# The last row block of an output projection, loaded in groups of 25 rows on a decode kernel

## The chip, the cores and the metric

The kernel runs on one core of a Trainium2 chip. The metric is device time in microseconds for one execution, the median of the runs. Five engines work side by side, each with its own instruction queue: TensorE (PE; its weight loads are shown as PEld), VectorE (DVE), ScalarE (ACT), GpSimd (POOL) and SyncE (SP). Sixteen DMA engines move data between HBM and SBUF; here SP issues the large loads and ACT a few tiny ones and the store. An instruction waits on semaphores, and a load raises its own semaphore as it lands, a step for each DMA engine that carried a share of it.

## The reference

One decode step for one token with D = 576: a layer norm, then two branches on the same normalised row, summed with the residual.

```python
xn = _layernorm(x)
# A: 32 query heads on 16 key/value heads, the last W = 4096 positions of the cache
q = xn @ wq                                  # 576 x 4096
p = softmax(q k^T * 128**-0.5)               # per head, 4096 keys
a = (p v) reshaped to 4096 @ wo              # 4096 x 576
# B: a gated MLP with one token
z = gelu(xn @ w_in)                          # 576 x 4608, halves z1, z2
b = (z1 * (w_sp * layernorm(z2) + b_sp)) @ w_out   # 2304 x 576
return x + a + b
```

All tensors are bfloat16. About 51 MB are read in one execution: the two caches' windows (16.8 MB each), wq, w_in, w_out and wo.

## The kernel before

The order of the work is written out by hand: every engine runs its instructions in the order in which the program names them. SP's queue is a list of loads. `rows` (L74 to L83) loads n row blocks of a weight matrix, `load_kv` (L85 to L89) four heads of a cache. A weight matrix with R rows lies in SBUF with R/128 consecutive rows to each of the 128 partitions, so that "row block" s is the 128 rows `p * (R/128) + s`, one to a partition. Four large buffers a, b, c, d (32 KB in each partition) are reused, and a load into one waits for the last reader of what was there.

SP's order is: wq in two loads, K0, K1, w_in in two, K2, V0, K3, V1, V2, V3, w_out, and then wo (32 row blocks, wo's row `32 p + s`) in five loads of 14, 9, 6, 2 and 1 blocks (L108), so that the last blocks can be used soon after they land. A row block of wo is 1152 bytes in a partition. Eight semaphores serve all the loads and the store in turn, so the ninth load waits for the first to have landed, and so on.

The stages: x is normalised (POOL computes the power -0.5, L203) and put into a stationary form `XT`; wq gives q, and a set of copies with masks spreads it as `Qb`. For each of four groups of four heads: `keys` transposes K on DVE (L264), `scores` multiplies on TensorE (L271), `sm_a` and `sm_b` do the softmax (exp on ACT, transposes on DVE, copies on ACT), `pv` multiplies with V, and `tail` normalises (`norm`), brings the result into columns with `y_mms` and copies it to `Y` (L363). `Y` has, for each of 32 row blocks of wo, a column of 128 values with a column of zeros on either side; a pair of columns is the stationary operand, so the output row falls into one of the two rows of an accumulator.

At the end, `out_mms` (L468 to L472) multiplies one row block with its column of `hv` (branch B) or `Y` (branch A): four matmuls of 144 columns, for the four quarters of the 576 outputs, into two accumulators `acc` of 2 x 144 that lie in different column groups of TensorE. Order on TensorE after the last `pv`: 12 blocks of w_out (`out_hv(0)`, `out_hv(1)`), the transposition of the last group's result, six more blocks of w_out, then the 32 blocks of wo in the order of their loads. DVE and ACT copy one accumulator each (L486, L487), and ACT issues the store (L488).

POOL clears tiles at the start (`pz` in L166 is the longest) and does the two powers.

Of the kernel before, what the change touches and what calls it, by code (L numbers as in the profile page):

```python
# [8 lines left out]
FP32 = mybir.dt.float32  # L9
BF16 = mybir.dt.bfloat16  # L10
# [4 lines left out]
D = 576  # L15
HQ = 32
HKV = 16
DH = 128
# [6 lines left out]
TP = W // 32  # L25
TC = TP // 2
NR = 98
NF = FH // 128
QW = D // 4
XP = D // 3  # L30
EPS = 1e-5
SCALE = DH ** -0.5
# [5 lines left out]
def kernel(  # L38
# [14 lines left out]
    nc = tc.nc  # L53
    P = nc.NUM_PARTITIONS
# [3 lines left out]
    big = ctx.enter_context(tc.tile_pool(name="big", bufs=1))  # L58
    const = ctx.enter_context(tc.tile_pool(name="const", bufs=1))
# [5 lines left out]
    ps_m = ctx.enter_context(tc.tile_pool(name="ps_m", bufs=1, space=bass.MemoryType.PSUM))  # L65
# [8 lines left out]
    def rows(slot, src, name, lo, n, at=None):  # L74

        w = src.shape[1]
        if at is None:
            t = big.tile([P, n * w], BF16, name=f"{name}{lo}", tag=slot)[:]
        else:
            t = slot[:, at:at + n * w]  # L80
        v = t.rearrange("p (s c) -> p s c", c=w)
        nc.sync.dma_start(v, src.rearrange("(p s) c -> p s c", p=P)[:, lo:lo + n, :])  # L82
        return [(lo + s, v[:, s, :]) for s in range(n)]  # L83

    def load_kv(slot, src, g, name):  # L85

        t = big.tile([P, TP * DH], BF16, name=f"{name}{g}", tag=slot)
        nc.sync.dma_start(t[:], src[0, GK * g:GK * g + GK, SK - W:SK, :].rearrange("h (r t) d -> r h (t d)", t=TP))
        return t[:].rearrange("p (t d) -> p t d", d=DH)  # L89

    wq_h = A_wq.rearrange("r (e c) -> (r e) c", e=2)
    win_h = B_w_in.rearrange("r (e c) -> (r e) c", e=2)
    K, V = {}, {}
    rest = big.tile([P, TP * DH], BF16, name="rest", tag="d")
    wq_sb = rows(rest, wq_h, "wq", 0, 2, 0) + rows("a", wq_h, "wq", 2, 7)
    K[0] = load_kv("b", A_k_cache, 0, "k")
    K[1] = load_kv("c", A_k_cache, 1, "k")
    win_sb = rows("a", win_h, "win", 0, 7) + rows(rest, win_h, "win", 7, 2, 4096)
    K[2] = load_kv("b", A_k_cache, 2, "k")
    V[0] = load_kv("c", A_v_cache, 0, "v")  # L100
    K[3] = load_kv("d", A_k_cache, 3, "k")
    V[1] = load_kv("a", A_v_cache, 1, "v")
    V[2] = load_kv("b", A_v_cache, 2, "v")
    V[3] = load_kv("c", A_v_cache, 3, "v")
    ends = [big.tile([P, TP * DH], BF16, name=f"end{n}", tag="ad"[n]) for n in range(2)]
    wout_sb = rows(ends[0], B_w_out, "wout", 0, NF, 0)
    wo_sb = []
    for n, t, at in ((14, 1, 0), (9, 1, 14), (6, 0, NF), (2, 0, NF + 6), (1, 0, NF + 8)):  # L108
        wo_sb += rows(ends[t], A_wo, "wo", len(wo_sb), n, at * D)


    xrow = const.tile([1, D], BF16, name="xrow")
    for n in range(3):
        nc.scalar.dma_start(xrow[:, XP * n:XP * (n + 1)], x_flat[:, XP * n:XP * (n + 1)])
    spb = const.tile([1, 2], BF16, name="spb")
# [4 lines left out]
    ident = const.tile([P, P], BF16, name="ident")  # L120
# [47 lines left out]
    for n in range(2):  # L168
        t = ps_s.tile([P, 2, 512], FP32, name=f"S{n}")
# [9 lines left out]
    nc.gpsimd.memset(mb[:], 0.0)  # L179

    xtw = const.tile([1, NS, D // NS, 2], BF16, name="xtw")
    nc.vector.tensor_copy(xtw[:], xrow[:].rearrange("p (m j) -> p j m", j=NS).unsqueeze(3).to_broadcast([1, NS, D // NS, 2]))  # L184
    for j in range(NS):
        nc.tensor.matmul(ps_x[:, j:j + 1], lhsT=xtw[:, j].rearrange("p m h -> p (m h)"), rhs=ones_b[:, 0:1],  # L186
                         start=True, stop=True)
# [30 lines left out]
    for s, wv in wq_sb:  # L218
        for g in range(4):
            nc.tensor.matmul(  # L220
                qps[32 * g:32 * g + 2, :], lhsT=XT[:, s, :], rhs=wv[:, 512 * g:512 * (g + 1)],
                start=(s == 0), stop=(s == NS - 1), tile_position=(0, 32 * g),
# [12 lines left out]
    for k in range(4):  # L235
        for be in range(4):
            nc.tensor.matmul(
                qps2[:, k, be, :].rearrange("p (r g) -> p r g", r=2),
                lhsT=q_rep[0:NR, 2 * k + be // 2, be % 2].rearrange("p a d -> p (a d)"),
                rhs=idq, start=True, stop=True)  # L240
# [10 lines left out]
    Y = const.tile([P, 32, 3], BF16, name="Y")  # L251
    nc.gpsimd.memset(Y[:], 0.0)
    hv = const.tile([P, NF, 3], BF16, name="hv")
    nc.gpsimd.memset(hv[:], 0.0)
    KT = {}
    st = {}

    def keys(g, c):
# [4 lines left out]
        for n in range(4):  # L263
            nc.vector.transpose(dst[:, 1024 * n:1024 * (n + 1)], src[:, 1024 * n:1024 * (n + 1)])  # L264
        KT[g, c] = kT

    def scores(g, c):
        kv = KT.pop((g, c))[:].rearrange("p (t s) b r x e -> p b e x t r s", s=2)
        for be in range(4):
            for x in range(GK):  # L270
                nc.tensor.matmul(  # L271
                    S[g % 2][32 * x:32 * x + 8, c, :],
                    lhsT=Qb[:, GK * g + x, be].rearrange("p a h -> p (a h)"),
                    rhs=kv[:, be // 2, be % 2, x],
                    start=(be == 0), stop=(be == 3), tile_position=(0, 32 * x),
                )
# [141 lines left out]
    def tail(g):  # L418
        recip(g)
        norm(g)  # L420
        y_mms(g)
        y_copy(g)
# [16 lines left out]
    acc = []  # L439
    for n, pool in enumerate((ps_a, ps_b)):  # L440
        t = pool.tile([P, 512], FP32, name=f"acc{n}", tag="ab"[n])
        acc.append(t[32 * n:32 * n + 2, 0:QW])
        for r in range(2):
            nc.tensor.matmul(acc[n], lhsT=one3[:, 1 - r:3 - r], rhs=xrow[:, QW * (2 * r + n):QW * (2 * r + n + 1)],
                             start=(r == 0), stop=False, tile_position=(0, 32 * n))
# [19 lines left out]
    sums(3)  # L465
    pv(3)

    def out_mms(lhs, col, wv, last):  # L468
        for r in range(2):
            for n in range(2):  # L470
                nc.tensor.matmul(acc[n], lhsT=lhs[:, col, 1 - r:3 - r], rhs=wv[:, QW * (2 * r + n):QW * (2 * r + n + 1)],  # L471
                                 start=False, stop=(last and r == 1), tile_position=(0, 32 * n))  # L472

    def out_hv(c):
        for t, wv in wout_sb[6 * c:6 * c + 6]:
            out_mms(hv, t, wv, False)

    out_hv(0)
    out_hv(1)
    tail(3)  # L480
    out_hv(2)
    for t, wv in wo_sb:
        out_mms(Y, t, wv, t == 31)

    res = const.tile([2, 2 * QW], BF16, name="res")
    nc.vector.tensor_copy(res[:, 0:QW], acc[0])  # L486
    nc.scalar.copy(res[:, QW:2 * QW], acc[1])  # L487
    nc.scalar.dma_start(out.rearrange("a b (r c) -> (a b r) c", r=2), res[:])  # L488
# [30 lines left out]
```

## Time and profile before

| | |
|---|---|
| median of 3 runs | 127.01 us (126.64 to 127.16) |
| the profiled execution | 126.97 us, span of its instructions 125.1 us |
| bytes read | 50.96 MB, 407 GB/s over the span |
| busy: PE, DVE, ACT, POOL | 70.2, 78.6, 43.2, 7.2 us |
| DMA packets | 2613, of those 2592 on SP's queue |
| mean granted TensorE clock | 0.754; 1.00 after 116 us |
| wo's one-block load, issue to landing | 31.2 us |

How to read it: times in the profile are microseconds from the first instruction. The page gives busy time by engine and in 40 equal slices, the DMA queues, the chain of work that ended last, and groups of instructions by source line. Further views list the instructions in order of time, who waited for whom, and busy time in chosen stretches: for each engine the busy time and the number of instructions, then the granted clock, the mean busy share of the 16 DMA engines, and GB/s. In a line such as `117.31 3.06 PE L471 ...` the first number is the start and the second the length; the brackets hold the idle time before it and what ended that. Beside these views the trace keeps a record of every DMA packet (queue, start, length, bytes) and of every step of a load's semaphore.

### The profile page before, as it was taken

Reading aid. Unit: us, or ns where it says so; the run is one execution under the profiler, and the core shown is the slowest. Engines: PE = TensorE matmul, PEld = TensorE weight load, DVE = VectorE, ACT = ScalarE, POOL = GpSimd, SP = SyncE. Lnnn points to the kernel's source line nnn. Section 1 sums busy time; section 2 is a strip of 40 time slices with the busy share of each in tenths; the row PEclk is TensorE's granted clock in tenths of the full one; section 3 lists DMA queues with packets and bytes.
Section 4 is the critical chain, followed back from the end, with each engine's and each line's share of the span. In section 5 each row is a group of like instructions: output and inputs, shape, how many; then the busy total and the mean of one; then the engine's idle time right before and its main releaser. Section 6 shows DMA issues by size and latency. Waiting matters only on the chain.

```text
span 125.1 us, 1826 instructions
## 1 busy us (share of the span) xinstructions
PE 70.2 (56%) x728; PEld 30.4 (24%) x728; DVE 78.6 (63%) x152; ACT 43.2 (34%) x101; POOL 7.2 (6%) x21
## 2 busy tenths in 40 slices
PE   0012841009886659999580991059892931059972
PEld 0011201001101002999100031002212311026961
DVE  6845135899699976509999367999938359003200
ACT  2100011000000974998079009608701941940000
POOL 2972000000000000000000000000000100000000
PEclk9999997555599958655568599558997555555999
DMA  4999899998999999898999989899998989999960
GB/s 113 507 422 440 363 503 409 430 482 356 498 389 433 385 482 471 377 492 341 492 430 419 471 367 487 359 482 440 409 482 356 492 374 453 414 434 409 413 248 0
DMA packets 2613, 51.06 MB, mean 408 GB/s; under 512 B 300, under 2 KB 430, under 8 KB 686
## 3 DMA queue, kind: packets, MB, share of 16 engines
q1 hardware_dynamic: 2592, 50.96, 95.3%
q8 instruction: 5, 0.08, 0.2%
q14 instruction: 2, 0.02, 0.0%
q10 hardware_dynamic: 14, 0.00, 0.0%
HBM read 50.96 MB, written 0.00 MB: 407 GB/s over the span
## 4 chain that ended last, share of the span: by engine, by line
DMA 62%; DVE 30%; PE 4%; SPq 1%; issue 1%; ACT 0%; DVEq 0%
DMA k<-in_A_k_cache_dram 36%; DMA end<-in_A_wo_dram 25%; DVE kT L264 22%; DVE pt L309 4%; PE S L271 3%; SPq L82 1%; DVE mx L292 1%; DVE on L349 1%; DVE om L345 1%; PE acc L471 0%; PE yps L356 0%; DVE rs L326 0%; ACT res L487 0%; DVE mt L281 0%; DVE mb L287 0%
## 5 line engine op out<-in xcount | busy, mean ns | idle before, releaser
L271 PE MATMUL S<-kT,Qb 128*8 128x512 bf16 x128 | 32.4, 1145 | 23.2 <-DVE kT L264 22.7
L264 DVE STREAM_TRANSPOSE kT<-k 128x1024 f32<-128x1024 f32 x32 | 36.8, 1207 | 6.2 <-DMA k<-in_A_k_cache_dram 6.2
L298 ACT ACTIVATE pz<-S,nm 32x1024 bf16<-32x1024 f32 x16 | 19.2, 1198 | 34.0 <-DVE nm L295 21.1
L312 ACT COPY PT<-pt 32x128 f32<-32x128 f32 x64 | 19.9, 311 | 16.5 <-DVE pt L309 15.8
L335 PE MATMUL ops<-v,PT 128*32 128x512 bf16 x128 | 11.0, 506 | 6.8 <-ACT PT L312 6.8
L271 PEld LDWEIGHTS <-Qb 128*8 128x8 bf16 x128 | 3.6, 96 | 44.9 <-issue 35.4
L309 DVE STREAM_TRANSPOSE pt<-pz 128x1024 f32<-128x1024 f32 x8 | 9.4, 1210 | 0.8 <-ACT pz L298 0.8
L345 DVE SCALAR_TENSOR_TENSOR om<-ops,rs,dmask 128x512 f32<-128x512 f32 x4 | 3.0, 751 | 10.5 <-PE ops L335 10.3
L371 PEld LDWEIGHTS <-win 128*128 128x128 bf16 x126 | 7.9, 166 | 2.0 <-issue 2.0
L371 PE MATMUL zps<-XT,win 128*128 128x2 bf16 x126 | 8.0, 202 | 0.0
L292 DVE TENSOR_REDUCE mx<-S 128x1 f32<-128x1024 f32 x4 | 4.9, 1216 | 4.0 <-PE S L271 3.9
L335 PEld LDWEIGHTS <-PT 128*32 128x32 bf16 x128 | 3.8, 118 | 11.4 <-ACT PT L312 6.9
L229 ACT CAST q_rep<-qps 128x512 bf16<-128x512 f32 x2 | 1.2, 585 | 14.9 <-DVE q_rep L231 14.9
L410 POOL TENSOR_TENSOR mz<-mz,mhalf 128x1 f32<-128x1 f32 x1 | 0.6, 553 | 84.9 <-DVE mz L409 84.9
L186 PE MATMUL ps_x<-ones_b,xtw 1*128 1x1 bf16 x9 | 0.4, 162 | 8.9 <-DVE xtw L184 8.9
L471 PE MATMUL acc<-end,Y 128*2 128x144 bf16 x128 | 4.5, 226 | 0.9 <-DMA end<-in_A_wo_dram 0.8
L231 DVE CAST q_rep<-qps 128x512 bf16<-128x512 f32 x2 | 1.4, 692 | 4.9 <-PE qps L220 4.2
L487 ACT CAST res<-acc 2x144 bf16<-2x144 f32 x1 | 0.3, 270 | 12.0 <-PE acc L471 12.0
L471 PEld LDWEIGHTS <-Y 128*2 128x2 bf16 x128 | 4.1, 84 | 1.2 <-issue 1.2
L356 PE MATMUL yps<-on,sel 128*32 128x32 f32 x32 | 2.0, 210 | 4.1 <-DVE on L349 4.1
L349 DVE TENSOR_REDUCE on<-om 128x128 f32<-128x512 f32 x4 | 4.2, 1043 | 0.1
L486 DVE CAST res<-acc 2x144 bf16<-2x144 f32 x1 | 0.3, 295 | 5.7 <-PE acc L471 5.7
(96 smaller groups left out, 57.6 us busy)
## 6 DMA issues: line engine op xcount, KB each, us to landing
k<-in_A_k_cache_dram SPq DMA_DIRECT2D x4, 4096.0 KB
v<-in_A_v_cache_dram SPq DMA_DIRECT2D x4, 4096.0 KB, 25.4
win<-in_B_w_in_dram SPq DMA_DIRECT2D x1, 4032.0 KB, 26.9
wq<-in_A_wq_dram SPq DMA_DIRECT2D x1, 3584.0 KB, 12.8
end<-in_B_w_out_dram SPq DMA_DIRECT2D x1, 2592.0 KB, 22.3
end<-in_A_wo_dram SPq DMA_DIRECT2D x1, 2016.0 KB
end<-in_A_wo_dram SPq DMA_DIRECT2D x1, 1296.0 KB
rest<-in_B_w_in_dram SPq DMA_DIRECT2D x1, 1152.0 KB
```

Of the source, the lines that this page charges most:

```text
L264: nc.vector.transpose(dst[:, 1024 * n:1024 * (n + 1)], src[:, 1024 * n:1024 * (n + 1)])
L271: nc.tensor.matmul(S[g % 2][32 * x:32 * x + 8, c, :], lhsT=Qb[:, GK * g + x, be].rearrange("p a h -> p (a h)"), rhs=kv[:, be // 2, be % 2, x],
L292: nc.vector.tensor_reduce(out=mx[:, 0:1], in_=s[:], op=ALU.max, axis=mybir.AxisListType.XY)
L298: nc.scalar.activation(pz[lo:hi, :, :, x, :], s[lo:hi].rearrange("p a (t r e) -> p (a t) r e", r=8, e=2), ACT.Exp, bias=nm[lo:hi, 0:1], sc ...
L309: nc.vector.transpose(dst[:, 1024 * n:1024 * (n + 1)], src[:, 1024 * n:1024 * (n + 1)])
L312: nc.scalar.copy(PT4[32 * a:32 * a + 32, :, x, :], pt[32 * x:32 * x + 32, :, 2 * a:2 * a + 2])
L335: nc.tensor.matmul(ops[32 * q:32 * q + 32, :], lhsT=d["PT"][:, t0 // 2:t0 // 2 + 2].rearrange("p t x h e -> p (t x h e)"), rhs=V[g][:, t0: ...
L345: nc.vector.scalar_tensor_tensor(out=om[:].rearrange("p c d -> p (c d)"), in0=ops[:], scalar=d["rs"][:, 0:1], in1=dmask[:].rearrange("p c ...
L349: nc.vector.reduce_sum(on[:], om[:].rearrange("p c d -> p d c"), axis=AXX)
L356: nc.tensor.matmul(yps[32 * g:32 * g + 32, :], lhsT=sel[:, dq, :], rhs=d["on"][:, 32 * dq:32 * dq + 32], start=(dq == 0), stop=(dq == 3), ...
L371: nc.tensor.matmul(zps[:, :, t], lhsT=wt[:, t, :], rhs=XT[:, s, :], start=(s == 0 and t == 0), stop=(s == NS - 1 and t == NF - 1), skip_gr ...
L471: nc.tensor.matmul(acc[n], lhsT=lhs[:, col, 1 - r:3 - r], rhs=wv[:, QW * (2 * r + n):QW * (2 * r + n + 1)], start=False, stop=(last and r ...
```

## The change

The last row block of wo (block 31) is no longer one load of 128 rows. Its first quarter of columns (144 of 576) comes with block 30, which lies just before it in memory: a load of 128 rows of 720 columns, 1440 bytes. Block 29 gets its own load, and is now the last block that TensorE multiplies. The other three quarters of block 31 (432 columns, 864 bytes a row) go to a tile `ext` of its own, with three slots of 432 columns: 125 of the 128 rows in five loads of 25 rows, to partitions 0 to 24 and 80 to 104 of the slots in turn, issued last of all on SP; the remaining three rows in loads of one row each, to partitions 80 to 82 of the third slot, issued early, between K1 and w_in. `ext` is cleared by POOL before that.

As row `i` of the block now lies in another partition, Y's column 31 has to follow. `move` holds three 128 x 128 matrices with a one for each row that moved and zeros elsewhere (POOL copies them out of the identity); three matmuls bring the column into three columns `yx`, DVE copies them to `Yx`, which has zeros on either side like `Y`. Each slot of `ext` is then multiplied with its column of `Yx`, three quarters each: nine matmuls. The partitions without a row have zeros on both sides.

`out_mms` is split so that one quarter can be issued alone (`out_mm`). The loads from w_in on stand further down in the source, behind the definition of `ext`; apart from the three small loads their order on SP is the same.

```diff
+XR = 25
+XB = 80
+XN = 3
...
-    for n, t, at in ((14, 1, 0), (9, 1, 14), (6, 0, NF), (2, 0, NF + 6), (1, 0, NF + 8)):
-        wo_sb += rows(ends[t], A_wo, "wo", len(wo_sb), n, at * D)
...
+    ext = const.tile([P, XN, D - QW], BF16, name="ext")
+    nc.gpsimd.memset(ext[:], 0.0)
+    last = A_wo.rearrange("(p s) c -> p s c", p=P)[:, 31, QW:D]
+    for i in range(P - 5 * XR):
+        nc.sync.dma_start(ext[XB + i:XB + i + 1, 2, :], last[5 * XR + i:5 * XR + i + 1])
+    win_sb = rows("a", win_h, "win", 0, 7) + rows(rest, win_h, "win", 7, 2, 4096)
...
+    for n, t, at in ((14, 1, 0), (9, 1, 14), (6, 0, NF)):
+        wo_sb += rows(ends[t], A_wo, "wo", len(wo_sb), n, at * D)
+    wo_p = A_wo.rearrange("(p s) c -> p (s c)", p=P)
+    at, w30 = (NF + 6) * D, D + QW
+    nc.sync.dma_start(ends[0][:, at:at + w30], wo_p[:, 30 * D:30 * D + w30])
+    row30 = ends[0][:, at:at + w30]
+    row29 = ends[0][:, at + w30:at + w30 + D]
+    nc.sync.dma_start(row29, wo_p[:, 29 * D:30 * D])
+    for j in range(5):
+        lo = XB * (j % 2)
+        nc.sync.dma_start(ext[lo:lo + XR, j // 2, :], last[XR * j:XR * j + XR])
...
+    Yx = const.tile([P, XN, 3], BF16, name="Yx")
+    nc.gpsimd.memset(Yx[:], 0.0)
+    move = const.tile([P, XN, P], BF16, name="move")
+    nc.gpsimd.memset(move[:], 0.0)
+    for j in range(6):
+        lo, n = XB * (j % 2), min(XR, P - XR * j)
+        nc.gpsimd.tensor_copy(move[:, j // 2, lo:lo + n], ident[:, XR * j:XR * j + n])
...
+    def out_mm(lhs, col, q, wv, last=False):
+        n, r = q % 2, q // 2
+        nc.tensor.matmul(acc[n], lhsT=lhs[:, col, 1 - r:3 - r], rhs=wv, start=False, stop=last,
+                         tile_position=(0, 32 * n))
+
+    def out_mms(lhs, col, wv, last=False):
+        for q in range(4):
+            out_mm(lhs, col, q, wv[:, QW * q:QW * (q + 1)], last and q >= 2)
...
+    yx = ps_m.tile([P, 32], FP32, name="yx", tag="m")
+    for j in range(XN):
+        nc.tensor.matmul(yx[:, j:j + 1], lhsT=move[:, j, :], rhs=Y[:, 31, 1:2], start=True, stop=True)
+    nc.vector.tensor_copy(Yx[:, :, 1], yx[:, 0:XN])
     for t, wv in wo_sb:
-        out_mms(Y, t, wv, t == 31)
+        out_mms(Y, t, wv)
+    out_mms(Y, 30, row30)
+    out_mm(Y, 31, 0, row30[:, D:D + QW])
+    for j in range(XN):
+        for q in range(1, 4):
+            out_mm(Yx, j, q, ext[:, j, QW * (q - 1):QW * q])
+    out_mms(Y, 29, row29, True)
```

More of the change, by code (lines that the diff above doesn't have):

```diff
@@ L97 @@
     K[1] = load_kv("c", A_k_cache, 1, "k")
[L98 to L107, printed above, removed]
-    for n, t, at in ((14, 1, 0), (9, 1, 14), (6, 0, NF), (2, 0, NF + 6), (1, 0, NF + 8)):
-        wo_sb += rows(ends[t], A_wo, "wo", len(wo_sb), n, at * D)
     xrow = const.tile([1, D], BF16, name="xrow")
@@ L179 @@
     nc.gpsimd.memset(mb[:], 0.0)
+    ext = const.tile([P, XN, D - QW], BF16, name="ext")
[4 more added lines that the diff above has]
+    win_sb = rows("a", win_h, "win", 0, 7) + rows(rest, win_h, "win", 7, 2, 4096)
+    K[2] = load_kv("b", A_k_cache, 2, "k")
+    V[0] = load_kv("c", A_v_cache, 0, "v")
+    K[3] = load_kv("d", A_k_cache, 3, "k")
+    V[1] = load_kv("a", A_v_cache, 1, "v")
+    V[2] = load_kv("b", A_v_cache, 2, "v")
+    V[3] = load_kv("c", A_v_cache, 3, "v")
+    ends = [big.tile([P, TP * DH], BF16, name=f"end{n}", tag="ad"[n]) for n in range(2)]
+    wout_sb = rows(ends[0], B_w_out, "wout", 0, NF, 0)
+    wo_sb = []
+    for n, t, at in ((14, 1, 0), (9, 1, 14), (6, 0, NF)):
[9 more added lines that the diff above has]
+        nc.sync.dma_start(ext[lo:lo + XR, j // 2, :], last[XR * j:XR * j + XR])
     xtw = const.tile([1, NS, D // NS, 2], BF16, name="xtw")
@@ L466 @@
     pv(3)
[L468 to L472, printed above, removed]
+    def out_mm(lhs, col, q, wv, last=False):
[5 more added lines that the diff above has]
+            out_mm(lhs, col, q, wv[:, QW * q:QW * (q + 1)], last and q >= 2)
     def out_hv(c):
         for t, wv in wout_sb[6 * c:6 * c + 6]:
-            out_mms(hv, t, wv, False)
+            out_mms(hv, t, wv)
     out_hv(0)
```

## The prediction

> **What bounds the kernel now.** I read the page first, part 2 (the span in 40 slices) and part 4 (the chain that ended last), then the chain in order of time, the timeline of the last ten microseconds, and busy time in stretches of a microsecond there.
>
> ```profile
> DMA  4999899998999999898999989899998989999960
> DMA 62%; DVE 30%; PE 4%; SPq 1%; issue 1%; ACT 0%; DVEq 0%
> ...
> 90.70 31.43 DMA end<-in_A_wo_dram
> 122.13 0.04 issue
> 122.17 0.61 PE acc L471 x12
> 122.78 0.02 issue
> 122.81 0.27 ACT res L487
> ```
>
> The 16 DMA engines are 90% busy or more in nearly every slice, and the chain ends in a load of `wo`, then 12 matmuls, the copy and the store. The loads are a stream that never stops, so only its last microseconds can be shortened.
>
> ```profile
> 117.31 3.06 PE L471 MATMUL acc<-end,Y 128*2 128x144 bf16 x92
> 121.14 1.60 PE L471 MATMUL acc<-end,Y 128*2 128x144 bf16 x36 [0.77 <-DMA end<-in_A_wo_dram]
> 121.14 0.77 PEld L471 LDWEIGHTS <-Y 128*2 128x2 bf16 x24 [0.92 <-issue]
> 122.17 0.36 PEld L471 LDWEIGHTS <-Y 128*2 128x2 bf16 x11 [0.26 <-issue]
> ...
> 119.00:120.00 1.00, 1.00 (x38) 1.00 (x34) 0.00 (x0) 0.00 (x0) 0.00 (x0) 1.00 0.97 393
> 120.00:121.00 1.00, 0.37 (x12) 0.23 (x7) 0.00 (x0) 0.00 (x0) 0.00 (x0) 1.00 0.64 237
> 121.00:122.00 1.00, 0.86 (x24) 0.77 (x24) 0.00 (x0) 0.00 (x0) 0.00 (x0) 1.00 0.26 85
> ```
>
> The reader is to see two things. First, the DMA share (the column before the last) falls to 0.64 and 0.26 from 120 on: most engines are done, some still work. Second, TensorE stands between two limits: it waits for the six-row load of `wo` until 121.14, then loads 24 weights in 0.77 us, waits only 0.26 us more (to 122.17) for the two-row load, and ends.
>
> The records of single DMA packets say who is late. A packet follows the last one on its engine 3 to 4 ns before that one's recorded end, so sixteen lanes can be followed, though without engine numbers. At 117.0 they stand, behind the first, at 0, 0.11 to 0.20 (six), 0.34, 0.35, 0.42, 0.55, 0.82, 1.46, 1.53, 1.58 and 1.62 us. Each late lane fell back at one instruction packet:
>
> ```profile
> q8 instruction: 5, 0.08, 0.2%
> q14 instruction: 2, 0.02, 0.0%
> ```
>
> Those of 16 KB start at 37.4, 57.2, 76.6, 100.7 and 120.1, each costs its lane 1.42 to 1.46 us, and no lane is hit twice; the two of 8 KB cost 0.55 and 0.8 us. The last hits the lane at 0.42. The semaphore increments of the last load run from 120.53 to 122.41, so ten lanes are through 1.1 to 1.9 us before the last one.
>
> **The change part by part.** The sum stands against the profiled execution, 126.97 us (span 125.1 and 1.9 around it); the median of the three runs is 127.01, so a forecast from it reads 0.04 low against the median.
>
> *Loads at the end.* Removed per lane: 8 packets of 2304 B (93 ns each) and 8 of 1152 B (51 ns). Put in: 8 of 1440 B and 8 of 1152 B. From 51 and 93 a packet costs 9 ns and 42 ns per 1152 B, less the 3 ns of overlap, so 1440 B take 58 against 90 ns. Every lane saves 8 x 32 = 0.25 us. Then come 125 packets of 864 B, 37 ns each. How many lanes carry 25 rows no row shows: 128 rows went to 16 lanes, 8 each, the two-row store to two, one-row loads to one. They are equal shares over as many lanes as allow it, up to 16; of 25 that is 5 lanes of 5 rows. Bounds: 16 lanes (nothing saved) and one lane (125 x 37 = 4.6 us on it). I take five, by that pattern: 25 x 37 ns + 5 increments of 6 ns = 0.96 us on each. An early lane ended its last packets at 120.2 to 120.6, now 0.25 earlier and 0.96 later: 120.95 to 121.4, and landed 0.3 after that, 121.3 to 121.7.
>
> [...]
>
> *TensorE's tail.* Removed after the six-row load: 12 matmuls. Put in: 5 from row 30 and the first quarter of row 31, 9 from the 25-row tile, 4 from row 29: 18. In the trace a pair on the two accumulators starts within 4 ns, the next pair 62 ns later, and a matmul on the same accumulator waits that long. The six-row load and its landing at 121.10 stay, and its 24 matmuls are issued by 121.89. From there the 18, in their order (the second accumulator comes twice in a row at two places), start over 0.56 us: the last at 122.45 if no load is late, against 122.52 in the trace. Do the loads come in time? The two-row load landed at 122.13, that of row 30 now by 121.88 (due 121.89); row 29 at 122.41 - 0.25 = 122.16 (due 122.33); the 25-row loads by 121.7 (due 122.01 to 122.26). So TensorE, not the stream, sets the end: **-0.07 us**, or -0.03 if row 30 is a moment late. Of the 0.25 us, six more matmuls take the rest.
>
> *Waits of the five loads.* SP issues them last. Each takes over the semaphore of an earlier load: those landed at 95.4, 105.0, 111.2, 115.9 and, for the last, 119.04 (the nine-row load of `wo`). The store was issued at 123.14 and its packets moved at 123.89; SP's first load took 1.0 us. So the fifth one's packets are ready by 119.8 to 120.1, and the five lanes reach them at 120.8 or later. Behind it SP has only the end of the program. Cost nothing; the cover is 0.7 us in the queue plus 0.3 us in TensorE.
>
> *TensorE ahead of the tail.* Three one-hot matmuls with 128 columns of weights, as in L371 (126 in 8.0 us, 63 ns each): 0.2 us from 117.25. TensorE idles 0.77 us before 121.14, so hidden. DVE's copy (like Y's, 0.21 us) falls in its idle time of 5.67 us.
>
> *POOL and the early rows.* Clearing the tile of 1296 columns comes before POOL's power for the mean (L203). `pz` with 4096 took 3.51 us, so 1.1 us, from 8.46 to 9.6; POOL idles 2.86 us there until 11.33. The one-hot work (a memset and six copies at 0.14 us, as `sel`'s, about 1.2 us) follows at 12.1, and POOL's next task is at 97. DVE's chain of L184 to L202 runs beside the memset; if it lost as much as 1 us, the cover is the scores, whose weights stood at 23.13 while the keys landed at 23.72. The three one-row loads are issued on SP by 11 us; the next issue, `win`, waits for TensorE until 17.16. Their packets, 0.13 us, follow K1 on one lane. That lane, which carried x's one-row loads, stands at 0.20; 0.33 is still early.
>
> Every other issue of SP waits for the same landings as before. Sum: 126.97 - 0.07 + 0.03 for row 30 = **126.93 us**.
>
> **The rivals.**
>
> *A late lane is among the five (slower).* Say one at 1.46 to 1.62, or the one hit at 120.1. Its row 29 ends 0.25 us earlier, the 25 packets 0.96 us later: landing 122.75 to 123.0. The last slot's three matmuls and row 29's four then start up to 0.2 us after that, so TensorE's last starts at 122.98 to 123.25 instead of 122.52: 127.45 to 127.7 us, most at 127.6. It decides from a lateness of about 1.0 us; lanes at 0.55 and 0.82 cost nothing. For it: five of 16 lanes are that late, and no record numbers them. [...]
>
> [...]
>
> *TensorE has room after all.* If the whole 0.25 us came through, 126.72 us. Against it: its issue at 62 ns a pair holds over all 92 matmuls before.
>
> *The 25 rows don't go to five lanes.* On 16 nothing is won, and 25 rows over 16 don't divide; 126.97 plus the six matmuls. On one lane, 4.6 us after about 120.0, landing near 125: 129.6 us.
>
> **How the numbers follow.** Forecast (TensorE bound, 126.7 to 127.05) 0.55; late lane 0.25; other lanes' partitions 0.10; all 0.25 us gained 0.05; 25 rows elsewhere 0.05. The time is that of the first, 126.93. The range runs from 126.55 (the full gain and 0.17 of scatter; the three runs lay 126.64 to 127.16) to 127.7, the upper end of the late lane; beyond lies the one-lane case. A measurement here tells about 0.5%, 0.63 us: faster by more needs under 126.38, which no case gives: 0.04. Slower by more needs over 127.65: half the late lane and the one-lane case: 0.18. Within: 0.78.
>
> **What would show it.** Right: 25-row loads whose semaphores count five increments and land before 121.9; the DMA share lower in 121 to 122; weight loads after 121.14 without the 0.26 us gap; the last matmul at about 122.45. Wrong: TensorE waiting for `ext` (late lane); row 30 landing after 122.0 (other lanes' partitions); `ext` landing near 125; SP's last issue after 120.

## The result and the profile after

The changed kernel takes 127.12 us (median of 8 runs, 127.05 to 127.26) against 126.80 us of the kernel before in the same comparison (8 runs, 126.64 to 127.16). The ratio is 1.0025, with a 95% interval of 1.0013 to 1.0037: slower by 0.3 us. That is inside the 0.5% that the prediction called no difference and inside its range (126.55 to 127.7), but 0.19 us above the forecast of 126.93, and on the other side of the kernel before: forecast was 0.04 us less than before, measured 0.32 us more.

The page of the changed kernel, parts 2 and 4, in the lines that answer to those shown of before:

```profile
DMA  4999899897998999899998989999899999999950
...
DMA 61%; DVE 28%; PE 7%; SPq 1%; issue 1%; ACT 0%; DVEq 0%
```

The end of its chain in order of time (start, length, what), and its timeline:

```profile
90.93 30.49 DMA end<-in_A_wo_dram
121.42 0.04 issue
121.46 1.55 PE acc L494 x42
123.01 0.02 issue
123.03 0.27 ACT res L524
```

```profile
116.92 0.14 PEld L511 LDWEIGHTS <-move 128*128 128x128 bf16 x3
117.19 0.16 DVE L512 CAST Yx<-yx 128x3 bf16<-128x3 f32 x1 [0.57 <-PE yx L511]
...
121.46 1.10 PE L494 MATMUL acc<-end,Y 128*2 128x144 bf16 x29 [0.96 <-DMA end<-in_A_wo_dram]
121.46 0.89 PEld L494 LDWEIGHTS <-Y 128*2 128x2 bf16 x28 [1.11 <-issue]
122.28 0.27 PEld L494 LDWEIGHTS <-Yx 128*2 128x2 bf16 x7
122.33 0.41 PE L494 MATMUL acc<-ext,Yx 128*2 128x144 bf16 x7
```

The remaining six matmuls (four of row 29 and two of `ext`) follow one or two to a line. The busy time in stretches of a microsecond (PE, PEld, DVE, ACT, POOL, then granted clock, DMA share, GB/s):

```profile
119.00:120.00 1.00, 0.79 (x26) 0.79 (x27) 0.00 (x0) 0.00 (x0) 0.00 (x0) 1.00 0.96 371
120.00:121.00 1.00, 0.50 (x16) 0.35 (x11) 0.00 (x0) 0.00 (x0) 0.00 (x0) 1.00 0.68 239
121.00:122.00 1.00, 0.54 (x18) 0.54 (x19) 0.00 (x0) 0.00 (x0) 0.00 (x0) 1.00 0.27 88
```

The chain now ends in another load. Before, it ran through the two-row load (122.13) and 12 matmuls; now it runs through the six-row load, landed at 121.42, and all 42 matmuls behind it. The weight loads have no gap any more, and the last matmul starts at 122.77, 1.31 us behind the first one. TensorE sets the end from the six-row landing on, as forecast; but that landing, 121.10 in the trace of before, came 0.32 us later.

### The profile page after: what moved, and what is told of

Same layout as the page of the kernel before. It is cut to its first block, busy times and chain, and to the rows that moved or that the text cites. A ratio compares the mean times of both kernels' runs of the same rounds, so it can differ in the third digit from the quotient of the medians.

```text
span 125.3 us, 1865 instructions
## 1 busy us (share of the span) xinstructions
PE 70.3 (56%) x737; PEld 30.8 (25%) x737; DVE 79.1 (63%) x153; ACT 43.1 (34%) x101; POOL 9.6 (8%) x30
## 4 chain that ended last, share of the span: by engine, by line
DMA 61%; DVE 28%; PE 7%; SPq 1%; issue 1%; ACT 0%; DVEq 0%
DMA k<-in_A_k_cache_dram 37%; DMA end<-in_A_wo_dram 24%; DVE kT L288 22%; DVE pt L333 4%; PE S L295 3%; PE ops L359 2%; SPq L85 1%; PE acc L494 1%; DVE on L373 1%; DVE om L369 1%; PE lps L342 0%; PE yps L380 0%; PE acc L468 0%; ACT res L524 0%; DVE u L404 0%
## 5 line engine op out<-in xcount | busy, mean ns | idle before, releaser
L359 PE MATMUL ops<-v,PT 128*32 128x512 bf16 x128 | 10.5, 484 | 6.8 <-ACT PT L336 6.8
```

The costliest lines, as they stand in the source:

```text
L359: nc.tensor.matmul(ops[32 * q:32 * q + 32, :], lhsT=d["PT"][:, t0 // 2:t0 // 2 + 2].rearrange("p t x h e -> p (t x h e)"), rhs=V[g][:, t0: ...
```

## The experiments

Three tables serve all of them. First, the times:

| kernel | median us (runs) | ratio to before, 95% |
|---|---|---|
| the change | 127.12 (8) | 1.0025, 1.0013 to 1.0037 |
| split6 | 127.09 (8) | 1.0030, 1.0018 to 1.0041 |
| tail128 | 126.96 (12) | 1.0016, 1.0007 to 1.0024 |
| xb32 | 127.30 (7) | 1.0041, 1.0026 to 1.0055 |
| early25 | 127.60 (6) | 1.0061, 1.0047 to 1.0074 |
| no_ext_mm | 126.91 (10) | 1.0005, 0.9992 to 1.0018 |
| no25 | 126.90 (10) | 1.0004, 0.9993 to 1.0014 |
| ext_first | 127.29 (8) | 1.0047, 1.0029 to 1.0065 |
| before_plus25 | 126.92 (11) | 1.0008, 0.9999 to 1.0017 |

The kernel before lay at 126.76 to 126.84 in these comparisons. The other runs (after_again, before_again, place0, place80, place80_again, two25, wide25) have one timed execution each and are used for their traces.

Second, the tail in the traces. "Landing" is the last semaphore step of the six-row load, then come how many matmuls follow it and when the last one starts, and what the end of the program takes after the store has landed:

| kernel | landing | matmuls behind | last starts | store landed | from there to the end |
|---|---|---|---|---|---|
| before | 121.10 | 36 | 122.52 | 124.26 | 0.84 |
| before_again | 121.22 | 36 | 122.39 | 124.14 | 0.84 |
| the change | 121.42 | 42 | 122.77 | 124.47 | 0.83 |
| after_again | 121.54 | 42 | 122.90 | 124.59 | 0.84 |
| tail128 | 121.16 | 36 | 122.43 | 124.13 | 0.93 |
| no_ext_mm | 121.26 | 33 | 122.30 | 124.05 | 0.83 |
| no25 | 121.39 | 33 | 122.43 | 124.19 | 1.08 |
| before_plus25 | 121.29 | 36 | 122.55 | 124.29 | 0.83 |

Third, the lag of the late lanes. In a lane's packets of a load the last one has 4 bytes; a step of the load's semaphore follows. The time between the two is called the lag here. On the four lanes that are last, the mean time from the start of that packet to the step was, for the nine-row load and the six-row load behind it:

| traces | nine rows | six rows |
|---|---|---|
| no 25-row loads behind: before, before_again, tail128, no25 | 0.37 to 0.39 | 0.36 to 0.38 |
| two 25-row loads: two25 | 0.39 | 0.46 |
| five: the change, after_again, xb32, no_ext_mm, before_plus25 | 0.36 to 0.38 | 0.46 to 0.57 |
| five with twice the bytes: wide25 | 0.38 | 0.57 |
| five, all to one place: place0, place80, place80_again | 0.38 to 0.39 | 0.62 to 0.70 |
| five, but ahead of wo, landed by 112: ext_first | 0.44 | 0.45 |

split6 and early25 have no six-row load and stand in no row.

**Both kernels once more.** No edit.

> The changed kernel once more, for a second trace. Theory T (the end is set by the landing of the six-row load of wo plus the 42 matmuls behind it, 1.31 us from the first start to the last): the last matmul again starts 1.31 us after the first one behind that landing, with no gap. Theory P (the 25-row writes delay the landings of the late lanes): the last four increments of the six-row load again come 0.42 to 0.58 us after their packets, where the kernel before has 0.33 to 0.40. If the second half of that was chance, they lie at 0.33 to 0.40 here and the landing is near 121.1 to 121.2.

> The kernel before once more, for a second trace, as its first profiled execution (126.97 us) was 0.2 us above the median of its runs (126.77). Theory T: the last matmul starts at 122.3 to 122.5, set by the landing of the last one-row load; increments of the late lanes come 0.33 to 0.40 us after their packets in the six-row load. If the first trace was typical in its tail, the last matmul starts at 122.5 again and the difference to the median lies before it.

The chains end so, first the changed kernel, then the kernel before:

```profile
121.54 0.04 issue
121.58 1.55 PE acc L494 x42
```

```profile
121.22 0.04 issue
121.27 1.39 PE acc L471 x36
```

The changed kernel repeats itself: 42 matmuls in one run, the last 1.31 us after the first. The kernel before doesn't. Its second trace has no 0.26 us gap: TensorE works through from the six-row landing, waits only for the one-row load (landed at 122.28, not 122.41) and its last matmul starts at 122.39. The room behind the six-row load that the prediction read in its one trace was mostly that execution's. That execution took 126.97 us, with a median of 126.80. Its packet records say what made the room. The lane that carried the instruction packet at 120.10 was pushed behind all others: its last packet of the one-row load starts at 121.96, 0.12 us after every other lane's. By the pattern of the steps, which is the same for the other lanes in both loads, its step is also the one that ends the two-row load at 122.13; the four late lanes were through at 121.80. In the second trace that packet came at 119.57, and the two-row load landed at 121.92.

**The six rows split.**

```diff
-    for n, t, at in ((14, 1, 0), (9, 1, 14), (6, 0, NF)):
+    for n, t, at in ((14, 1, 0), (9, 1, 14), (4, 0, NF), (2, 0, NF + 4)):
```

> The six-row load of wo is split into four rows and two rows, all else as in the changed kernel. Theory T: only 8 + 18 matmuls (0.81 us) are left behind the landing at about 121.4, so the end goes back to the last load (row 29, 122.3): last matmul at 122.35 to 122.45 instead of 122.77, time 0.3 to 0.4 us below the changed kernel, 126.7 to 126.8. Rival S (the stream of loads as a whole got later, TensorE is not the bound): no change, 127.1.

Four rows landed at 120.58, so TensorE had 16 matmuls fewer behind the last of the six (landed at 121.34). What replaced them was a new wait. With one more load every semaphore moves on by one, and the fifth 25-row load now takes over that of the four-row load: SP could issue it only behind 120.58.

```profile
111.33 9.52 SPq L198 DMA_DIRECT2D ext<-in_A_wo_dram  x4
```

```profile
121.34 0.04 issue
121.38 0.41 PE acc L494 x8
121.79 0.03 issue
121.83 0.44 PE acc L494 x8
122.28 0.61 PE acc L494 x10
```

The first line is SP's timeline (issues of four of the five, the last ending at 120.85), the others the chain. That load landed at 122.42 and its matmuls waited for it. The last matmul started at 122.65, 0.13 us earlier than in the trace of the changed kernel, and the store landed 0.13 us earlier too; the end of the program took the gain back (1.08 us after the store, against 0.83). The median is the same, 127.09, where 126.7 to 126.8 was expected.

**The 25-row loads ahead.** In early25 they stand behind the nine-row load, in ext_first behind w_out; in both their nine matmuls come before those of the last six rows, and early25 splits the six as well.

```diff
-    for n, t, at in ((14, 1, 0), (9, 1, 14), (6, 0, NF)):
+    for n, t, at in ((14, 1, 0), (9, 1, 14)):
+        wo_sb += rows(ends[t], A_wo, "wo", len(wo_sb), n, at * D)
+    for j in range(5):
+        lo = XB * (j % 2)
+        nc.sync.dma_start(ext[lo:lo + XR, j // 2, :], last[XR * j:XR * j + XR])
+    for n, t, at in ((4, 0, NF), (2, 0, NF + 4)):
```

> The five loads of 25 rows are issued right behind the nine-row load of wo, ahead of the six rows, which are split into four and two; TensorE does the nine matmuls of the moved rows behind the nine rows. Bytes, packets and lanes as in split6. Theory T: behind the landing of the two rows (121.2 to 121.5) stand 8 + 9 matmuls, 0.53 us, and the end is row 29's landing (122.0 to 122.3) plus 0.1: last matmul at 122.1 to 122.4 and 126.5 to 126.8 us, below the changed kernel by 0.3 to 0.6 and at or below the kernel before. Rival S (the loads in groups of 25 slow the stream wherever they stand): 127.0 to 127.2.

```diff
     wout_sb = rows(ends[0], B_w_out, "wout", 0, NF, 0)
+    for j in range(5):
+        lo = XB * (j % 2)
+        nc.sync.dma_start(ext[lo:lo + XR, j // 2, :], last[XR * j:XR * j + XR])
...
-    for t, wv in wo_sb:
+    for t, wv in wo_sb[:23]:
         out_mms(Y, t, wv)
...
+    for t, wv in wo_sb[23:]:
+        out_mms(Y, t, wv)
```

> The changed kernel with the five loads of 25 rows issued behind w_out's load, ahead of the 14 rows of wo, so that they land by 113 and no later load waits for a late semaphore; TensorE does the nine matmuls of the moved rows behind the nine-row load, in its idle time before the six rows. Bytes, packets and lanes are those of the changed kernel. Theory T (the end is the six-row landing plus the matmuls behind it): 33 matmuls, 1.00 us, are left, and the 25-row writes are over by then, so that landing is at 121.1 to 121.25 with increments 0.33 to 0.42 us after their packets; end set by row 29, landing at 122.05 to 122.25: last matmul 122.2 to 122.35, 126.6 to 126.8 us, 0.3 to 0.5 below the changed kernel. Rival S (the groups of 25 cost the stream wherever they stand): 127.0 to 127.2. Rival W (the changed kernel's semaphore waits on SP, not its matmuls): also lower here, but then the last matmul stands right behind row 29's landing and that landing itself is earlier than 122.28.

Both were expected at or below the kernel before. early25 is clearly slower than the change; ext_first is 0.17 us slower, with intervals that overlap. The chain of early25 shows the semaphores again, now on SP's large loads:

```profile
119.71 0.33 SPq L197
120.04 0.04 issue
120.08 2.96 DMA end<-in_A_wo_dram
123.04 0.04 issue
123.08 0.33 PE acc L496 x4
```

L197 issues row 30, and waits for the nine-row landing of 119.70; row 29 is issued at 120.08 and lands 2.96 us later, on every lane after 122.4. In ext_first the six-row load waits in the same way for w_out:

```profile
89.02 22.74 DMA end<-in_B_w_out_dram
111.78 9.99 DMA end<-in_A_wo_dram
121.77 0.04 issue
121.81 1.31 PE acc L494 x33
```

That delay cost nothing by itself: the late lanes went on from the nine rows to the six without a pause (2.08 us from the last packet of the one to that of the other, as in the other traces). But more lanes than four are late now: the extra packets of the five lanes (0.94 us on one lane in the trace of the change) lie ahead of the six-row load, which landed at 121.77, and row 29 at 122.58 (122.28 in the change). So of these places, the one behind all other loads, where the change has them, is the best.

**One load of 128 rows in place of the five.** Row 29 before it, three matmuls of 128 rows with Y's own column; no one-hot matmuls, no early rows.

```diff
-    for j in range(5):
-        lo = XB * (j % 2)
-        nc.sync.dma_start(ext[lo:lo + XR, j // 2, :], last[XR * j:XR * j + XR])
+    nc.sync.dma_start(ext[:], last)
...
-    out_mms(Y, 29, row29, True)
+    out_mms(Y, 29, row29)
+    for q in range(1, 4):
+        out_mm(Y, 31, q, ext[:, QW * (q - 1):QW * q], q >= 2)
```

> The order of the last loads as in the changed kernel, but the three quarters of block 31 come as one load of 128 rows behind row 29; no moved column, no one-hot work, 12 matmuls behind the six rows instead of 18. Theory T: TensorE has 36 matmuls behind the six-row landing (1.12 us) and the end is the last load again, about 122.45 as in the kernel before: 126.8 to 126.9. Theory P: the last increments of the six-row load come 0.33 to 0.40 us after their packets. Rival S: as slow as the changed kernel, 127.1, as its order of loads is the same.

```profile
118.82 1.92 PE L482 MATMUL acc<-end,Y 128*2 128x144 bf16 x56
121.20 1.22 PE L482 MATMUL acc<-end,Y 128*2 128x144 bf16 x33 [0.47 <-DMA end<-in_A_wo_dram]
122.37 0.28 PE L482 MATMUL acc<-ext,Y 128*2 128x144 bf16 x3
```

With 36 matmuls again, and the last load landing at 122.33, the time is 126.96: 0.16 us less than the change. The traces show more: the store landed 0.34 us earlier, and 0.10 us of that was given back at the end of the program (0.93 against 0.83). It is still 0.19 us slower than the 126.77 of the kernel before in the same comparison, clear of the interval. The end of the program accounts for 0.10 us of that; what makes the rest is open.

**Parts of the change taken away, or alone.** no_ext_mm:

```diff
-    for j in range(XN):
-        for q in range(1, 4):
-            out_mm(Yx, j, q, ext[:, j, QW * (q - 1):QW * q])
```

> The nine matmuls of the moved rows are left out, loads and all else as in the changed kernel (the output lacks their part). Theory T: 33 matmuls behind the six-row landing, 0.28 us fewer: last matmul 0.28 us earlier relative to that landing, bounded by row 29's landing; 126.8 to 126.9. Rival S: 127.1.

no25 leaves out the five loads and the one-hot work too:

```diff
-    for j in range(5):
-        lo = XB * (j % 2)
-        nc.sync.dma_start(ext[lo:lo + XR, j // 2, :], last[XR * j:XR * j + XR])
...
-    for j in range(XN):
-        nc.tensor.matmul(yx[:, j:j + 1], lhsT=move[:, j, :], rhs=Y[:, 31, 1:2], start=True, stop=True)
-    nc.vector.tensor_copy(Yx[:, :, 1], yx[:, 0:XN])
```

> The five loads of 25 rows, the one-hot work and the nine matmuls are left out (the output lacks their part); the three one-row loads, row 30 and row 29 stay. Theory P (the 25-row writes make the late lanes' landings later): the last four increments of the six-row load come 0.33 to 0.40 us after their packets and it lands at 121.15 to 121.25, against 121.42 and 121.54 with the loads; time 126.6 to 126.75. If the lag has another cause (the three one-row loads, the tile's place in memory), it stays at 0.42 to 0.63 and the time is that of no_ext_mm.

before_plus25 is the kernel before with `ext` cleared, the three early rows, and the five loads, which nobody reads (its lines against the kernel before):

```diff
+    for i in range(P - 5 * XR):
+        nc.sync.dma_start(ext[XB + i:XB + i + 1, 2, :], last[5 * XR + i:5 * XR + i + 1])
...
+    for j in range(5):
+        lo = XB * (j % 2)
+        nc.sync.dma_start(ext[lo:lo + XR, j // 2, :], last[XR * j:XR * j + XR])
```

> The kernel before, with the changed kernel's clearing of the tile, its three one-row loads and its five loads of 25 rows added at the same places of SP's queue, and nothing that reads them; TensorE's work is that of before. It carries 0.11 MB more. Theory P (the 25-row writes make the late lanes' landings later): increments of the six-row load 0.42 to 0.6 us after their packets, landing 0.1 to 0.2 us later than before, time 126.85 to 127.0. If the loads cost nothing: 126.75 to 126.8, and the whole difference of the change is TensorE's six extra matmuls. If they cost all of it: 127.1.

The chains of no_ext_mm, no25 and before_plus25:

```profile
121.26 0.04 issue
121.30 1.27 PE acc L494 x33
```

```profile
121.39 0.04 issue
121.44 1.27 PE acc L484 x33
```

```profile
121.29 0.04 issue
121.33 1.49 PE acc L481 x36
```

The nine matmuls are worth 127.12 - 126.91 = 0.21 us; 33 matmuls take 1.00 us from the first start to the last, 42 take 1.31. (Each set against the kernel before of its own comparison, 126.80 and 126.76, it is 0.17 us.) no25, expected at 126.6 to 126.75, has the same time as no_ext_mm. In its trace the end of the program is 0.25 us longer, because its store has another semaphore (last section); two25, whose store comes one place later in that order, shows 0.20 us. Without that no25 would be at 126.65 to 126.70, and the five loads cost 0.21 to 0.26 us in the changed kernel. This is worked out, not measured: no run has no25's loads with the store on the semaphore of the change, and the landings of the two single traces (121.39 in no25, 121.26 in no_ext_mm) lie the other way, as no25's packets ran late in that execution (the latest lane's last at 120.97, against 120.71). In the kernel before, the loads cost 126.92 - 126.84 = 0.08 us, with an interval that includes zero. Both can hold, since TensorE works without a gap from the six-row landing on in the changed kernel, while the kernel before also waits for a later load; but this is argued and not shown.

**Where the rows go, and how many.** xb32 puts the second group of rows at partitions 32 to 56 (`XB = 32`); place0 sends all five loads to partitions 0 to 24 of five slots, place80 to 80 to 104; two25 keeps two of the loads, wide25 doubles their columns. All but xb32 leave out the nine matmuls and the one-hot work. place0 and place80 together ask whether the lag grows with one of the two places or with any loads of 25 rows.

```diff
-XB = 80
+XB = 32
```

> The second place of the 25-row loads is partitions 32 to 56 instead of 80 to 104, nothing else. Theory P with the late lanes among those that fill partitions 64 to 127: their increments come 0.33 to 0.40 us after the packets again, the six-row load lands 0.1 to 0.2 us earlier and the time falls by as much, to 126.9 to 127.0. If the writes' place doesn't matter: 127.1 and 0.42 to 0.58 us as before.

```diff
-        lo = XB * (j % 2)
-        nc.sync.dma_start(ext[lo:lo + XR, j // 2, :], last[XR * j:XR * j + XR])
+        nc.sync.dma_start(ext[0:0 + XR, j, :], last[XR * j:XR * j + XR])
```

> All five loads of 25 rows go to partitions 0 to 24 (five slots), the three rows to 64 to 66; the one-hot work and the nine matmuls are left out (the output lacks their part), as in no25, which had the increments of the six-row load 0.36 to 0.42 us after the packets. [...] If any 25-row loads do it, all late lanes lag alike in both.

For place80 the new line has `ext[80:80 + XR, j, :]`.

> As place0, with all five loads to partitions 80 to 104 and the three rows to 0 to 2. [...] If any 25-row loads do it: all alike, as in place0. If neither lags: it took both places or the tile's matmuls.

> Left out: the nine matmuls of the 25-row tile and the one-hot matmuls; all five 25-row loads go to partitions 80 to 104. The first run of this kernel had TensorE at half its clock after 122 us and a last late lane at 121.86. If these partitions get in the way of the late lanes, the increments of the six-row load lag longer than with all loads to partitions 0 to 24 (0.55 to 0.73 us), the landing again at 121.6 or later; if the place doesn't matter, lag 0.4 to 0.7 and landing 121.3 to 121.55 as there. If the halved clock belongs to TensorE's longer idle time, it shows again; if it was chance, the matmuls run at 62 ns a pair and the time is 126.9 to 127.0.

```diff
-    for j in range(5):
+    for j in range(2):
```

> Left out: the nine matmuls of the 25-row tile, the one-hot matmuls, and three of the five 25-row loads (two stay, to partitions 0 to 24 and 80 to 104). On the four late lanes the increment of the six-row load came 0.33 to 0.42 us after the lane's last packet in the traces without 25-row loads, and 0.41 to 0.73 (mean 0.52) with five of them. If it is the traffic that runs beside it that lengthens this, the lanes' extra work now ends at about 120.9 instead of 121.4 and the lag falls back to 0.37 to 0.42, the six-row landing to about 121.2; if it is the presence of such loads at all, the lag stays at 0.5 and the landing at 121.4. Last matmul 1.0 us behind the landing: 122.2 or 122.4; time 126.7 or 126.9.

```diff
-        nc.sync.dma_start(ext[lo:lo + XR, j // 2, :], last[XR * j:XR * j + XR])
+        nc.sync.dma_start(ext[lo:lo + XR, j // 2, :], wo_p[XR * j:XR * j + XR, 32 * D - 2 * (D - QW):32 * D])
```

> Left out: the nine matmuls of the 25-row tile and the one-hot matmuls; the five 25-row loads stay but with 864 columns instead of 432, so that each packet is twice as long and the five lanes work until about 122.2. If traffic beside them lengthens the late lanes' increments, those of the six-row load lag by 0.5 us or more and those of rows 30 and 29, which lay behind the extra work before, lag longer too (0.6 or more), the six-row landing at 121.4 to 121.6; if the number of loads or increments does it, the lag is as with 432 columns, 0.5 us on the six rows and no longer on rows 30 and 29. Last matmul 1.0 us behind the landing unless row 29 lands after 122.3; time 126.9.

xb32 was no faster (127.30), and its six-row landing (121.55) lags by 0.57 us as in after_again. place0 and place80_again lag alike, 0.64 and 0.62 us, with landings at 121.55 and 121.49; the first run of place80 has 0.70 us and 121.86. There one lane's step came 0.93 us behind its packet, and one packet of that lane took 0.44 us instead of 0.26. So the lag does not need partitions 80 to 104, though with one or two traces of each a smaller effect of the place can't be excluded. Where all rows go to one place, the lag was longer than with two in turn, in the three traces that there are. The time of place80's first run, 128.18 us, tells nothing of this: its granted clock fell to 0.51 at about 122, behind the six-row landing, and 33 matmuls took nearly twice as long (the chain, and a stretch of its windows).

```profile
121.86 0.04 issue
121.90 2.15 PE acc L486 x33
```

```profile
122.00:123.00 1.00, 1.00 (x22) 1.00 (x20) 0.00 (x0) 0.00 (x0) 0.00 (x0) 0.51 0.01 2
```

Repeated, the clock stood at 1.00 there and the time was 127.02, so the halved clock was that execution's. two25 and wide25 stand at the ends of the range of the five loads, 0.46 and 0.57 us (landings 121.26 and 121.45), in one trace each. The lag is there with two loads, 0.46 and not 0.37, and doubling the bytes gives no more than five loads of the plain size had in two of five traces. wide25's rows 30 and 29, still beside the longer loads, lag by 0.50 to 0.58 us on three of the late lanes, no longer than the six rows. So a lag of 0.46 us and more goes with 25-row loads that run at the same time. ext_first, where they were over by 112, stands between, with 0.44 and 0.45 us and more late lanes than the others. The time of the last instruction packet does not explain it: that started at 119.54 to 120.35 in the four traces without the loads, and at 119.66 to 119.82 in the five with 0.46 to 0.57. How the lag depends on the traffic these traces don't settle.

## Why the prediction was right in part, and where it was wrong

Forecast was a time 0.04 us below the kernel before, measured one 0.32 us above it. The step that failed is the six-row landing, which the prediction kept where it was; the base of the sum, a trace with more slack than the next one, was mis-sized as well. Most of the other steps held.

*25 rows lie on five lanes: right, but their landings were later than forecast.* Each of the loads raised its semaphore by five steps (the first at 120.72 to 121.47), as the author had estimated from the shares of the other loads. None of the five lanes is one of those 1.4 us or more late (those lanes' steps of row 29, which is issued ahead of the 25 rows, came at 121.96 and later, and the first of the five loads was in by 121.47), so the rival with the second largest chance did not happen. The loads landed at 121.47, 121.66, 121.88, 122.07 and 122.25 (forecast: by 121.7 for all), against due times that moved to 122.3 and later with the six-row landing; TensorE did not wait for them. Two signs that the prediction named did not show: two of the five loads landed after 121.9, and the DMA share from 121 to 122 is 0.27, not below the 0.26 of before.

*What was to be hidden: right.* The one-hot matmuls start at 116.92 and DVE's copy took 0.16 us, both long before the next landing. Clearing the tile took POOL 1.18 us from 8.40 (forecast 1.1 from 8.46). SP's last issue ended at 119.44, ahead of the 119.8 to 120.1 that was allowed for packets, and stood behind the nine-row landing as named.

*Rows 30 and 29: right in kind.* They landed at 121.96 and 122.28 (forecast 121.88 and 122.16), 122.01 and 122.33 in the second trace, and neither was waited for.

*"From there the 18 ... start over 0.56 us", TensorE sets the end: right.* From the six-row landing to the start of the last matmul the forecast had 122.45 - 121.10 = 1.35 us; measured 122.77 - 121.42 = 1.35.

*"The six-row load and its landing at 121.10 stay": this step failed.* It landed at 121.42 and 121.54, against 121.10 and 121.22 in the two traces of before. TensorE being the bound, every bit of that is in the time. The late lanes' packets came later by no more than the scatter between executions: the latest lane's last packet started at 120.84 and 120.91 in the two traces of the changed kernel, at 120.74 and 120.83 in those of before, and at 120.97 in no25. What grew is the lag, in the mean of the four late lanes from 0.37 us to 0.48 and 0.57, and on the lane that steps last from 0.36 and 0.39 to 0.58 and 0.64. The nine-row load a moment earlier, with all lanes at work, lags by 0.36 to 0.38 in the same traces. So the lag of the last lane accounts for about 0.2 us; the medians without the loads make it 0.21 to 0.26, with the allowance for the end of the program. The prediction had only asked whether the five lanes' own landings would be late, and whether their writes delay row 30; it put the effect of the new loads on the six-row load at nothing, without a reason.

*The base was mis-sized.* -0.07 us was counted from a trace with 0.26 us of idle time of TensorE at its end. The second trace of before has none of it at that place, and starts its last matmul 0.13 us earlier. In that trace the last matmul starts 1.17 us behind the six-row landing, so the 1.35 us of the change are 0.18 us more, where the prediction counted 0.07 us less. So a typical execution had less to win: the forecast of 126.93 is already 0.13 us above the median of 126.80. The prediction had the instruction packet of 120.10 in its list (it puts it on the lane at 0.42; by the packets it was the one at 0.35), and did not ask what it did to the two-row and one-row landings of 122.13 and 122.41, on which its slack and its due times rest.

*The rival of the other lanes' partitions (0.10)* had row 30 landing after 122.0 as its sign. It landed at 121.96 and 122.01, and was not waited for. Which partitions a lane writes no record shows. That partitions 80 to 104 in particular are the cause is refuted by xb32 and place0, which write elsewhere and lag as long (0.57 and 0.64 us). That the late lanes are held up by these loads' writes wherever they go is not refuted, and is near to what the lag shows. Between the places no clear difference was seen (0.64 us with all rows at 0 to 24, 0.70 and 0.62 at 80 to 104).

Put together from medians: 126.76 for the kernel before, -0.11 for the shorter stream and three matmuls fewer (no25, less 0.25 at its end), +0.26 for the loads beside (no_ext_mm against no25), +0.21 for the nine matmuls, gives 127.12. As each term is the difference of two neighbouring medians, the sum comes out of itself and proves nothing; it only says how the 0.3 us divide. The second and third terms rest on the allowance of 0.25 us, which no25's trace shows (two25's gives 0.20). What in the hardware makes the step of a semaphore later is open.

## What to carry to other kernels

Where the last loads are trimmed, look which engine stands behind the last *large* load: here the work that was moved behind that landing (six more matmuls, 0.2 us) was paid in full, though the trimmed loads were not waited for. Read the slack at the end of a kernel from more than one execution; here one trace had 0.26 us of it and the next none, as an instruction packet came 0.5 us later in the first. With semaphores that serve loads in turn, adding or moving one load changes what the later issues wait for (in split6 the fifth 25-row load could be issued only behind the landing at 120.58).

## What the runs showed that was not expected

*The late lanes' last step came later with 25-row loads beside it*: 0.36 to 0.39 us behind the last packet in the kernels without 25-row loads, 0.46 to 0.70 with such loads beside, 0.44 to 0.45 where they were over.

*The end of the program depends on which semaphore the store got.* SP waits at the end for the eight load semaphores in an order that is the same in the traces of before and of the change, about 64 ns for each wait. In the changed kernel only one wait was left when the store landed (124.48); in no25 there were four (124.25, 124.32, 124.38, 124.44), and its end took 1.08 us instead of 0.83. two25 had four as well (1.03 us), tail128 two (0.93 us). split6 had two waits and lost the rest in a later step of the end, of whose cause the records say nothing. Differences of 0.1 to 0.25 us between kernels with another number of loads can come from this alone.

*A load of one block that is issued late lands late*: in the one trace of early25, row 30 (issued at 119.71) needed 1.95 us from its issue to its first step and 2.62 us to its last, row 29 (issued at 120.08) 2.4 and 2.96 us, at a DMA share of 0.70 and 0.69 from 120 to 122.
